# Order of transposes, stores, loads and casts at the end of block 0 and in the two batches after it

## The chip, the cores and the metric

The kernel runs on one core of one Trainium2 chip. The metric is the device time of one execution in microseconds (us): the median of several runs. One more execution is taken by the hardware profiler, and all durations of single instructions come from it. TensorE is PE here, VectorE DVE, ScalarE ACT, GpSimd POOL, and SyncE, which only issues DMAs, SP.

## The reference

A retention layer over 8 batches, 8 heads, 576 tokens and a head size of 64, and then a feed-forward layer with a snake activation on all 4608 tokens:

```python
scores = (1/8) * q @ k.T
ret = (scores * Dmat) @ v          # Dmat[h, i, j] = gamma_h ** (i - j) for i >= j, else 0
x = ret, as 4608 tokens by 512 (batch and position by head and size)
h = x @ w_in                       # 512 by 2048
s = sin(alpha * h)
g = h + s * s / (alpha + 1e-9)
out = g @ w_out                    # 2048 by 512
```

Inputs and output are float32.

## The kernel before, in words

Each batch b has an object `at[b]` that does its retention for the first 512 tokens in two halves p of 256; the last 64 tokens of all batches come at the end as block 8. The 512 outputs of a batch, turned so that the features lie on the partitions (`xT`), are block n of the feed-forward layer. Retention of batch n+1 is woven into the feed-forward work of block n.

For one batch and half: `load` (SP, line 121) brings q, k or v in float32, 512 KB each, into one of six buffers. `cast` (line 181 for q and k, 102 or 104 for v) makes float16 on DVE, ACT or POOL and multiplies in powers of gamma. q and k must be turned so that the head size lies on the partitions (`qT`, `kT`). That is done in one of two ways: on PE with `turn` (line 215, eight 128x128 transposes into a PSUM bank) and two copies `take` (lines 102 and 104), as for batches 0 and 1; or, from batch 2 on, with `crossed` (line 205), a DMA transpose that SP issues. `scores` (line 363) and `masked` (line 375, DVE) make the masked scores, `outer` (line 298) the sums of k and v, `take_sum` and `next_sum` (102, 327), `more` (344, 345) and `to_state` (332) the running state, `values` (line 406) and `add_states` (428) the output, which `keep` (102 or 104) writes to `xT`. The two parts of `values` use the rows of PE in turns at one bank, so the second must come after the first: either PE drains, or an engine relays it. With `relay=A_` an empty instruction on ACT waits for the last matmul of the first part, and the second part waits for ACT (line 250).

For one block and one of 16 columns fc of 128: `project` (line 541) is four matmuls into a bank, `sine` (549, ACT), `square` (558 on ACT, 560 on DVE or POOL), and `product` (565, DVE), which writes `gT` and frees the bank. In blocks 0 and 1 the second matrix follows as `gemm2(n, u, bank)` (line 587): u is 4c + part, c one of four groups of 128 tokens, and part a quarter of w_out: each call multiplies by the four rows fk = 4 part to 4 part + 3, and four calls make one result, which `finish` copies (102 or 104) and SP stores (line 580, two stores of 128 KB). So `gemm2(0, 4)` and `gemm2(0, 12)` and `gemm2(0, 0)` use w_out's first quarter, `gemm2(0, 5)` and `gemm2(0, 13)` the second. The quarters come by `load_w_out(g)`, issued by POOL (line 95) ahead of its squares. `weigh` and the class `Quarters` serve blocks 2 to 8, which make the second product with seven multiplications instead of eight.

The order of the work is written out by hand: each engine's instructions, DMA issues too, stand in the order of the calls, and an instruction that must wait holds up all behind it on its engine. `told(x, eng)` is an empty instruction on `eng` that waits for x. Two of them matter here: POOL waits for the second half of `cast(1, "k", 0)` on DVE, and SP waits for `at[1].masked(0, 0)` ahead of the loads of batch 2.

PSUM has eight banks: h0, h1, h2, op of one bank each and m0, m1 of two. `project(0, 11, "op")` and then `gemm2(0, 4, "op")` use the same bank, so the second waits for `product(0, 11)`; `project(0, 12, "h2")` and `gemm2(0, 12, "h2")` likewise with `product(0, 12)`.

Of the kernel before, what the change touches and what calls it, by code (L numbers as in the profile page):

```python
# [18 lines left out]
def kernel(  # L19
# [68 lines left out]
    V, A_, G_ = nc.vector, nc.scalar, nc.gpsimd  # L88
# [5 lines left out]
    def load_w_out(g):  # L94
        nc.gpsimd.dma_start(w_out16[:, 4 * g : 4 * g + 4, :], w_out_r[:, 4 * g : 4 * g + 4, :])
# [42 lines left out]
    def cast(b, nm, p, eng, ys=(0, 1)):  # L138
        t_ = raw[b, nm, p]
        if (b, nm, p) not in half:  # L140
            if p < 2:
                if nm == "k":
                    d_ = work.tile([P, 16 * D], F16, tag=f"k16{slot(b, p)}", bufs=1, name="k16")
                elif nm == "q":
                    n = order_of_q.index((b, p)) % 3 if b < 5 else 1 - p
                    d_ = work.tile([P, 16 * D], F16, tag=f"q16{n}", bufs=1, name="q16")
                else:
                    d_ = work.tile([P, 16 * D], F16, tag="v16", bufs=4, name="v16")
                d_ = (
                    d_.rearrange("p (h r d) -> p h r d", r=2, d=D)  # L150
                    if nm == "v"
                    else d_.rearrange("p (a r t d) -> p a r t d", a=4, r=2, t=2)
                )
            elif nm == "v":
                d_ = work.tile([P, H, D], F16, tag="vs16", bufs=B // 2, name="vs16")
            else:
                tag, n = ("qks16", 2) if b % 4 == 0 else (f"k16{int(nm == 'q')}", 1)
                d_ = work.tile([P, 4, 2, D], F16, tag=tag, bufs=n, name=nm + "s16")
            half[b, nm, p] = d_
        dst = half[b, nm, p]  # L160
        if p == 2:
            if nm == "v":
                copy(eng, dst.rearrange("p h d -> p (h d)"), t_.rearrange("p h d -> p (h d)"))
            else:
                eng.tensor_tensor(
                    dst.rearrange("p a t d -> p t a d"),
                    t_.rearrange("p (t a) d -> p t a d", t=2),
                    fac_s[nm].rearrange("p (t a) -> p t a", t=2).unsqueeze(3).to_broadcast([P, 2, 4, D]),
                    MULT,
                )  # L170
        elif nm == "v":
            h0, h1 = 4 * ys[0], 4 * ys[-1] + 4
            copy(
                eng,
                dst[:, h0:h1].rearrange("p h r d -> p (h r d)"),
                t_[:, h0:h1].rearrange("p h x -> p (h x)"),
            )
        else:
            a0, a1 = 2 * ys[0], 2 * ys[-1] + 2
            n = 2 * (a1 - a0)  # L180
            return eng.tensor_tensor(  # L181
                dst[:, a0:a1].rearrange("p a r t d -> p t (a r) d"),
                t_.rearrange("p (t a) x -> p t a x", t=2)[:, :, a0:a1].rearrange("p t a (r d) -> p t (a r) d", r=2),
                fac["halved k" if nm == "k" and b >= HALVED else nm]
                .rearrange("p (t x) -> p t x", t=2)[:, :, 2 * a0 : 2 * a1]
                .unsqueeze(3)
                .to_broadcast([P, 2, n, D]),
                MULT,
            )
# [19 lines left out]
    def turn(b, nm, p, tag, ys=(0, 1)):  # L209
        if (b, nm, p) not in trs:  # L210
            trs[b, nm, p] = psum.tile([P, 1024], F16, tag=tag, bufs=1, name="tr")
        tr, x = trs[b, nm, p], half[b, nm, p]
        for a in range(2 * ys[0], 2 * ys[-1] + 2):
            for r in range(2):
                matmul(
                    tr[:, 256 * a + 128 * r : 256 * a + 128 * r + 128],
                    x[:, a, r].rearrange("p t d -> p (t d)"),
                    ident,
                    start=(a == 0 and r == 0), stop=True, is_transpose=True, skip_group_check=True,
                )  # L220

    def take(b, nm, p, eng, ys=(0, 1)):
        d_ = new_T(b, nm, p).rearrange("p x n -> p (x n)")
        cols = slice(512 * ys[0], 512 * ys[-1] + 512)
        copy(eng, d_[:, cols], trs[b, nm, p][:, cols])
# [22 lines left out]
    def told(last, eng):  # L248

        mark = eng.nop()  # L250
        order(mark, last)
        return mark
# [280 lines left out]
    def project(n, fc, tag, part=None):  # L533

        if n not in gT:
            gT[n] = work.tile([P, 2, FC, 256], F16, tag="gT", bufs=2, name="gT")
        if (n, fc) not in hps_of:
            hps_of[n, fc] = [bank(tag), None]
        cols = PART[part]
        for a in range(KT):  # L540
            matmul(  # L541
                hps_of[n, fc][0][:, cols], w_in16[:, a, fc * P : (fc + 1) * P], xs[n][:, a, cols],
                start=(a == 0 and part != 1), stop=(a == KT - 1), skip_group_check=True,
            )
# [9 lines left out]
    def square(n, fc, eng):  # L554
        s_t = hps_of[n, fc][1]
        ss_t = work.tile([P, 512], F16, tag="ss", bufs=4, name="ss_t")
        if eng is nc.scalar:
            nc.scalar.activation(ss_t, s_t, mybir.ActivationFunctionType.Square)  # L558
        else:
            eng.tensor_tensor(ss_t, s_t, s_t, MULT)  # L560
        hps_of[n, fc][1] = ss_t

    def product(n, fc):
        hps, ss_t = hps_of.pop((n, fc))
        nc.vector.scalar_tensor_tensor(  # L565
            gT[n][:, :, fc, :], ss_t.rearrange("p (t n) -> p t n", t=2), inva[:, fc : fc + 1],
            hps.rearrange("p (t n) -> p t n", t=2), MULT, ADD,
        )
# [7 lines left out]
    def finish(n, c, eng=None, cols=slice(0, 512), issue=(nc.sync, nc.sync)):  # L576
        osb = work.tile([P, 512], F32, tag="osb", bufs=4, name="osb")
        copy(eng or nc.scalar, osb[:, cols], ops[n, c, cols.start][:, cols])
        for r in range(2):
            issue[r].dma_start(rows_of(n, c)[r, :, cols], osb[halves(r), cols])  # L580

    def gemm2(n, u, tag, cols=slice(0, 512)):
        c, part = divmod(u, 4)
        if (n, c, cols.start) not in ops:
            ops[n, c, cols.start] = psum.tile([P, 512], F32, tag=tag, bufs=1, name="ops")
        for fk in range(4 * part, 4 * part + 4):
            matmul(  # L587
                ops[n, c, cols.start][:, cols], gT[n][:, c // 2, fk, c % 2 * P : c % 2 * P + P], w_out16[:, fk, cols],
                start=(fk == 0), stop=(fk == FC - 1), skip_group_check=True,
            )  # L590
# [102 lines left out]
    at = [Attention(b) for b in range(B)]  # L693
# [52 lines left out]
    with tc.manual_schedule():  # L746
# [139 lines left out]
        project(0, 10, "m0")  # L886
        sine(0, 10)
        square(0, 10, G_)
        told(cast(1, "k", 0, V, (1,)), G_)
        project(0, 11, "op")  # L890
        sine(0, 11)
        square(0, 11, A_)
        product(0, 10)
        product(0, 11)
        project(0, 12, "h2")
        sine(0, 12)
        square(0, 12, G_)
        project(0, 13, "h0")
        sine(0, 13)
        square(0, 13, A_)  # L900
        cast(1, "q", 0, G_)
        load_w_out(2)
        load_w_out(3)
        product(0, 12)
        project(0, 14, "h1")
        sine(0, 14)
        square(0, 14, A_)
# [1 line left out]
        project(0, 15, "m1")  # L909
        sine(0, 15)  # L910
        square(0, 15, A_)
        gemm2(0, 4, "op")
        turn(1, "k", 0, "m0")
        take(1, "k", 0, V, (0,))
        take(1, "k", 0, V, (1,))
        product(0, 14)
        product(0, 15)
        gemm2(0, 12, "h2")
        gemm2(0, 0, "h0")
        turn(1, "q", 0, "m0")  # L920
        take(1, "q", 0, A_, (0,))
        take(1, "q", 0, A_, (1,))
        at[0].to_state(3, G_)
        gemm2(0, 5, "op")
        gemm2(0, 13, "h2")
        at[1].scores(0, 0, "m0")
        at[1].scores(0, 1, "m1")
# [42 lines left out]
        at[1].outer((1,), "m0")  # L970
        at[1].next_sum(2)
        at[1].to_state(2, V)
        at[1].take_sum(3, A_)
        at[1].values(1, False, "m1", relay=A_)
        gemm2(0, 7, "op")
        at[1].values(1, True)
        at[1].add_states(1)
        at[1].keep(1, A_)
        finish(0, 1)
        cast(2, "k", 1, V, (1,))  # L980
        cast(2, "k", 0, V)
        crossed(2, 0, "k")
        crossed(2, 1, "k")
        at[1].more(3)
        at[1].to_state(3, G_)
        cast(2, "v", 0, G_)
# [13 lines left out]
        product(1, 0)  # L1000
        cast(2, "q", 0, V)
        crossed(2, 0, "q")
        load(3, "k", 1)
        finish(0, 0)
        square(1, 1, A_)
        project(1, 2, "m1", 0)
        project(1, 2, "m1", 1)
# [3 lines left out]
        project(1, 3, "h0")  # L1011
        sine(1, 3)
        crossed(2, 1, "q")
        load(3, "q", 1)
        load(3, "v", 0)
        load(3, "k", 0)
# [99 lines left out]
        sine(1, 15)  # L1116
        cast(3, "v", 1, A_, (0,))
        cast(3, "k", 0, V, (1,))
        load(4, "k", 0)
        crossed(3, 0, "k")  # L1120
        cast(3, "v", 0, G_, (0,))
        cast(3, "v", 1, G_, (1,))
        at[2].more(3)
# [390 lines left out]
```

## Time and profile before

| what | value |
|---|---|
| time, median of 3 runs | 295.11 us (294.53 to 295.81) |
| the profiled execution: its own time | 296.25 us |
| the profiled execution: span from first to last instruction | 294.5 us |
| PE busy | 280.7 us, 95% |
| DVE, ACT, POOL busy | 217.1, 211.3, 207.9 us |
| granted clock of PE | 1.0 throughout |
| DMA queue of SP (q1) | 114528 packets, 45.04 MB |
| DMA queue of POOL (q0) | 4224 packets, 4.19 MB |

Times in the views are us from the start of the span. A row of a timeline is start, length, engine, line, operation, output and inputs with their shapes, count, and in brackets the idle time ahead of it and what ended it. A row of the chain of waits is start, length, what. A row of a stage is its bounds, its length, then the busy time of PE, PEld (weight loads), DVE, ACT and POOL with their counts, then the granted clock, the mean busy share of the 16 DMA engines (it can pass 1 where packets overlap), and GB/s.

### The profile page before, as it was taken

The page shows a single profiled execution, that of the slowest core. Times are in us where ns is not written, and L with a number is a line of the kernel's source. Part 1 is how long each engine was busy: PE and PEld are TensorE (multiplying, and loading weights), DVE is VectorE, ACT ScalarE, POOL GpSimd, SP SyncE. Part 2 cuts the span into 40 slices and gives each one's busy share as a digit, 9 for nine tenths or more (in the row PEclk, how much of TensorE's full clock was granted, in tenths as well). Part 3 has the DMA queues.
Part 4 walks back from the last instruction along what each step waited for, and adds up shares of the span by engine and source line. Part 5 has one row for each costly group of instructions (what it writes and reads, how often), then busy time and mean ns, then how long its engine had stood idle before and what let it go on. Part 6 is the DMA issues. An engine that isn't in the chain of part 4 may idle for free.

```text
span 294.5 us, 8771 instructions
## 1 busy us (share of the span) xinstructions
PE 280.7 (95%) x3611; PEld 184.3 (63%) x3611; DVE 217.1 (74%) x299; ACT 211.3 (72%) x343; POOL 207.9 (71%) x198
## 2 busy tenths in 40 slices
PE   6799999989799999999999999999999999999993
PEld 5574455566544666676666666666666666665782
DVE  3859859999666689989686967686778495747861
ACT  3859733976849898787777778787868879887600
POOL 4888868999999989999997799679915800460000
PEclk9999999999999999999999999999999999999999
DMA  7999999999997887978798785778657101311225
GB/s 225 291 250 223 280 238 296 215 188 296 224 261 249 112 191 175 273 181 184 175 251 165 164 231 129 93 162 182 141 114 168 43 4 38 71 38 27 59 47 119
DMA packets 119159, 49.89 MB, mean 169 GB/s; under 512 B 69824, under 2 KB 118096, under 8 KB 119120
## 3 DMA queue, kind: packets, MB, share of 16 engines
q1 hardware_dynamic: 114528, 45.04, 65.2%
q0 software_dynamic: 4224, 4.19, 8.6%
q8 instruction: 28, 0.46, 0.7%
q10 hardware_dynamic: 368, 0.11, 0.2%
q14 instruction: 11, 0.09, 0.1%
HBM read 36.74 MB, written 9.44 MB: 157 GB/s over the span
## 4 chain that ended last, share of the span: by engine, by line
PE 75%; POOL 7%; DVE 6%; DMA 4%; ACT 3%; issue 2%; SPq 1%; ACTq 0%; POOLq 0%
PE hps L541 32%; PE hps L658 29%; PE ops L587 6%; DVE gT L565 2%; POOL T L608 2%; PE o L406 2%; PE sc L363 2%; DMA k<-in_k_dram 2%; DVE ret L375 2%; DMA qT<-q 2%; DVE k L181 2%; ACT s_t L549 1%; SPq L121 1%; POOL q L181 1%; PE kv L298 1%
## 5 line engine op out<-in xcount | busy, mean ns | idle before, releaser
L565 DVE SCALAR_TENSOR_TENSOR gT<-ss_t,inva,hps 128x512 f16<-128x512 f16 x144 | 105.2, 744 | 41.0 <-ACT ss_t L558 39.3
L549 ACT ACTIVATE s_t<-hps,alpha_t 128x512 f16<-128x512 f32 x144 | 96.5, 681 | 37.4 <-PE hps L541 37.0
L541 PE MATMUL hps<-xT,w_in 128*128 128x512 f16 (+1 forms) x604 | 121.3, 347 | 0.3
L541 PEld LDWEIGHTS <-w_in 128*128 128x128 f16 x668 | 63.7, 98 | 50.4 <-issue 1.2
L558 ACT ACTIVATE ss_t<-s_t 128x512 f16<-128x512 f16 x121 | 75.7, 630 | 3.4
L658 PEld LDWEIGHTS <-gT 128*128 128x128 f16 x656 | 63.9, 98 | 14.5
L630 POOL TENSOR_TENSOR gT<-gT,d 128x1024 f16<-128x1024 f16 x12 | 25.6, 2151 | 26.7 <-PE hps L658 26.0
L658 PE MATMUL hps<-T,gT 128*128 128x256 f16 x336 | 39.8, 273 | 0.0
L375 DVE TENSOR_TENSOR ret<-sc,mask 128x1024 f16<-128x1024 f32 (+1 forms) x32 | 35.0, 1119 | 6.4 <-PE sc L363 6.4
L658 PE MATMUL hps<-w_out,gT 128*128 128x256 f16 x320 | 38.2, 273 | 0.0
L678 DVE TENSOR_TENSOR osb<-osb,hps 128x512 f32<-128x512 f32 x35 | 24.0, 685 | 12.6 <-PE hps L658 11.3
L587 PE MATMUL ops<-w_out,gT 128*128 128x512 f16 x128 | 30.8, 380 | 0.7 <-DVE gT L565 0.7
L636 POOL TENSOR_TENSOR gT<-gT 128x1024 f16<-128x1024 f16 x12 | 25.3, 2128 | 0.0
L181 POOL TENSOR_TENSOR q<-q,cn 128x1024 f16<-128x1024 f32 (+1 forms) x16 | 25.2, 1590 | 0.1
L332 POOL TENSOR_TENSOR s<-kvs,cn 128x256 f16<-128x256 f32 x22 | 14.6, 664 | 8.2 <-ACT kvs L102 7.4
L587 PEld LDWEIGHTS <-gT 128*128 128x128 f16 x128 | 11.8, 98 | 13.1 <-issue 0.9
L345 POOL TENSOR_TENSOR kvs<-s,kvs 128x256 f32<-128x256 f32 x23 | 18.7, 812 | 1.8
L181 POOL TENSOR_TENSOR k<-k,cn 128x1024 f16<-128x1024 f32 (+1 forms) x11 | 18.8, 1709 | 0.0
L102 ACT COPY osb<-hps 128x512 f32<-128x512 f32 (+2 forms) x15 | 8.2, 549 | 13.5 <-PE hps L658 13.3
L102 ACT CAST xT<-o 128x1024 f16<-128x1024 f32 (+1 forms) x14 | 13.8, 989 | 4.0 <-PE o L428 4.0
L344 POOL TENSOR_TENSOR s<-kvs,cn 128x256 f32<-128x256 f32 x23 | 15.5, 673 | 1.6 <-DVE kvs L327 1.4
L541 PE MATMUL hps<-xS,w_in 128*128 128x512 f16 x64 | 15.0, 379 | 0.0
(78 smaller groups left out, 271.1 us busy)
## 6 DMA issues: line engine op xcount, KB each, us to landing
out_dram<-osb SPq DMA_DIRECT2D x70, 128.0 KB, 2.5
q<-in_q_dram SPq DMA_DIRECT2D x16, 512.0 KB, 6.0
k<-in_k_dram SPq DMA_DIRECT2D x10, 512.0 KB, 5.8
v<-in_v_dram SPq DMA_DIRECT2D x10, 512.0 KB, 6.6
k<-in_k_dram SPq DMA_DIRECT2D x24, 128.0 KB, 3.4
v<-in_v_dram SPq DMA_DIRECT2D x24, 128.0 KB, 3.6
w_in<-in_moe_w_in_dram POOLq DMA_DIRECT2D x4, 512.0 KB, 9.1
w_out<-in_moe_w_out_dram POOLq DMA_DIRECT2D x4, 512.0 KB, 9.5
```

The costliest lines, as they stand in the source:

```text
L102: eng.copy(d_, s_)
L181: return eng.tensor_tensor(dst[:, a0:a1].rearrange("p a r t d -> p t (a r) d"), t_.rearrange("p (t a) x -> p t a x", t=2)[:, :, a0:a1].rea ...
L375: made = nc.vector.tensor_tensor(ret.rearrange("p t (z x) -> p (t z) x", z=2)[:, :, 0:n], sc.rearrange("p t (z x) -> p (t z) x", z=2)[:, : ...
L541: matmul(hps_of[n, fc][0][:, cols], w_in16[:, a, fc * P : (fc + 1) * P], xs[n][:, a, cols], start=(a == 0 and part != 1), stop=(a == KT - ...
L549: nc.scalar.activation(s_t, hps, mybir.ActivationFunctionType.Sin, bias=0.0, scale=alpha_t[:, fc : fc + 1],)
L558: nc.scalar.activation(ss_t, s_t, mybir.ActivationFunctionType.Square)
L565: nc.vector.scalar_tensor_tensor(gT[n][:, :, fc, :], ss_t.rearrange("p (t n) -> p t n", t=2), inva[:, fc : fc + 1], hps.rearrange("p (t n) ...
L587: matmul(ops[n, c, cols.start][:, cols], gT[n][:, c // 2, fk, c % 2 * P : c % 2 * P + P], w_out16[:, fk, cols], start=(fk == 0), stop=(fk ...
L630: eng.tensor_tensor(self.part(0, 0, i), self.part(1, 1, i), self.d3[:, 4 * i : 4 * i + 4], SUB)
L636: eng.tensor_tensor(out_, self.part(1, 0, i), self.part(0, 0, i), SUB)
L658: matmul(self.ps[name][:, 256 * m + cols.start : 256 * m + cols.stop], left(j)[:, P * m : P * m + P], right(j)[:, cols], start=(tag is not ...
L678: nc.vector.tensor_tensor(out_, a, self.ps[ps], ADD)
```

## The change

Three groups of moves; no instruction is added or removed but for one copy that goes from ACT to DVE.

Block 0's end: the second half of `cast(1, "k", 0)` on DVE, and POOL's wait for it, move from ahead of products 11 and 10 to behind product 12; product 11 comes ahead of product 10; `load_w_out(2)` comes ahead of that wait, behind square 12; `gemm2(0, 12)` and `gemm2(0, 5)` come ahead of the turn of k, product 14 too; the second take of q goes to DVE.

On DVE, before (from its 16th row on; `k_635` is the cast k of batch 1, the rows of line 565 are products, the first of them up to product 9):

```order
L565 SCALAR_TENSOR_TENSOR gT<-ss_t,inva,hps 128x2x256 x9
L181 TENSOR_TENSOR k_635<-k_361,cn 128x2x4x64 x2
L565 SCALAR_TENSOR_TENSOR gT<-ss_t,inva,hps 128x2x256 x4
L104 COPY kT<-tr 128x512 x2
L565 SCALAR_TENSOR_TENSOR gT<-ss_t,inva,hps 128x2x256 x2
L375 TENSOR_TENSOR ret<-sc,mask 128x1024 x2
```

and now:

```order
L565 SCALAR_TENSOR_TENSOR gT<-ss_t,inva,hps 128x2x256 x9
L181 TENSOR_TENSOR k_635<-k_361,cn 128x2x4x64
L565 SCALAR_TENSOR_TENSOR gT<-ss_t,inva,hps 128x2x256 x3
L181 TENSOR_TENSOR k_635<-k_361,cn 128x2x4x64
L565 SCALAR_TENSOR_TENSOR gT<-ss_t,inva,hps 128x2x256 x2
L104 COPY kT<-tr 128x512 x2
L565 SCALAR_TENSOR_TENSOR gT<-ss_t,inva,hps 128x2x256
L104 COPY qT<-tr 128x512
L375 TENSOR_TENSOR ret<-sc,mask 128x1024 x2
```

Three products now stand between the two halves of the cast, and a copy of qT ahead of the mask product.

Batch 1's end: the first part of `at[1].values(1)`, with its relay on ACT, comes ahead of `take_sum(3)` on ACT. 

Batches 2 and 3, the queue of SP. Before (from its 19th row on; the stores are those of `finish(0, 3)`, `finish(0, 1)` and, the third pair, `finish(0, 0)`; `k_1100` and `k_999` are the cast k of batch 2, halves 0 and 1, `q_1155` and `q_1114` its q, `k_1159` the first load of batch 3):

```order
L580 DMA out_dram<-osb 64x512 x4
L205 DMA_TRANSPOSE kT<-k_1100 128x8x128
L205 DMA_TRANSPOSE kT<-k_999 128x8x128
L205 DMA_TRANSPOSE qT<-q_1155 128x8x128
L121 DMA k_1159<-in_k_dram 128x8x128
L580 DMA out_dram<-osb 64x512 x2
L205 DMA_TRANSPOSE qT<-q_1114 128x8x128
```

and now, where half 0 is `k_1096` and `q_1153`, half 1 `k_999` and `q_1112`, and the load is `k_1188`:

```order
L580 DMA out_dram<-osb 64x512 x2
L205 DMA_TRANSPOSE kT<-k_1096 128x8x128
L580 DMA out_dram<-osb 64x512 x2
L205 DMA_TRANSPOSE qT<-q_1153 128x8x128
L580 DMA out_dram<-osb 64x512 x2
L205 DMA_TRANSPOSE kT<-k_999 128x8x128
L205 DMA_TRANSPOSE qT<-q_1112 128x8x128
L121 DMA k_1188<-in_k_dram 128x8x128
```

Half 0's transposes have moved up past two stores and past half 1's k, and the load has moved down past a pair of stores and half 1's q. In batch 3 the transpose of k, half 0, comes ahead of the first load of batch 4.

The diff, with the calls around it:

```diff
         square(0, 10, G_)
-        told(cast(1, "k", 0, V, (1,)), G_)
         project(0, 11, "op")
         sine(0, 11)
         square(0, 11, A_)
+        product(0, 11)
         product(0, 10)
-        product(0, 11)
         project(0, 12, "h2")
         sine(0, 12)
         square(0, 12, G_)
+        load_w_out(2)
+        product(0, 12)
+        told(cast(1, "k", 0, V, (1,)), G_)
         project(0, 13, "h0")
         sine(0, 13)
         square(0, 13, A_)
         cast(1, "q", 0, G_)
-        load_w_out(2)
         load_w_out(3)
-        product(0, 12)
...
         square(0, 15, A_)
+        product(0, 14)
         gemm2(0, 4, "op")
+        gemm2(0, 12, "h2")
+        gemm2(0, 5, "op")
         turn(1, "k", 0, "m0")
         take(1, "k", 0, V, (0,))
         take(1, "k", 0, V, (1,))
-        product(0, 14)
         product(0, 15)
-        gemm2(0, 12, "h2")
         gemm2(0, 0, "h0")
         turn(1, "q", 0, "m0")
         take(1, "q", 0, A_, (0,))
-        take(1, "q", 0, A_, (1,))
+        take(1, "q", 0, V, (1,))
         at[0].to_state(3, G_)
-        gemm2(0, 5, "op")
         gemm2(0, 13, "h2")
...
         at[1].to_state(2, V)
+        at[1].values(1, False, "m1", relay=A_)
         at[1].take_sum(3, A_)
-        at[1].values(1, False, "m1", relay=A_)
...
         at[1].keep(1, A_)
-        finish(0, 1)
         cast(2, "k", 1, V, (1,))
         cast(2, "k", 0, V)
         crossed(2, 0, "k")
-        crossed(2, 1, "k")
+        finish(0, 1)
...
         crossed(2, 0, "q")
-        load(3, "k", 1)
         finish(0, 0)
+        crossed(2, 1, "k")
...
         crossed(2, 1, "q")
+        load(3, "k", 1)
         load(3, "q", 1)
...
         cast(3, "k", 0, V, (1,))
+        crossed(3, 0, "k")
         load(4, "k", 0)
-        crossed(3, 0, "k")
```

## The prediction

> **What bounds the kernel now.** First the page's line of busy times: it says which engine has no room to spare.
>
> ```profile
> PE 280.7 (95%) x3611; PEld 184.3 (63%) x3611; DVE 217.1 (74%) x299; ACT 211.3 (72%) x343; POOL 207.9 (71%) x198
> ```
>
> PE is busy for 280.7 of 294.5 us. A change that leaves PE's instructions alone, as this one does, can only give back PE's waits or add to them. The view of waits, PE alone, lists them for the whole run; the rows that lie in the part of the program that the change touches:
>
> ```profile
> PE sc L363 <- DMA qT<-q: 2.5, 2, 1.5
> PE ops L587 <- DVE gT L565: 0.7, 1, 0.7
> PE o L406 <- ACTq L250: 0.2, 1, 0.2
> ```
>
> The columns are total, times, longest. Together 3.4 us, 1.1% of the span: that is all that can be won, and the last of them ends at 80.16 us. Behind that PE has no wait that the view names, so what PE gains or loses by 80 us is carried to the end.
>
> **Where the four waits stand.** The timeline of PE:
>
> ```profile
> 32.35 1.02 PE L587 MATMUL ops<-w_out,gT 128*128 128x512 f16 x4 [0.66 <-DVE gT L565]
> 50.09 0.42 PE L406 MATMUL o<-ret,v 64*64 64x128 f16 x16 [0.15 <-ACTq L250]
> 59.52 1.92 PE L541 MATMUL hps<-xT,w_in 128*128 128x256 f16 x16
> 62.45 0.42 PE L363 MATMUL sc<-qT,kT 64*64 64x128 f16 x16 [1.01 <-DMA qT<-q]
> 77.95 0.71 PE L298 MATMUL kv<-v,k 64*64 64x64 f16 x64
> 80.16 0.42 PE L363 MATMUL sc<-qT,kT 64*64 64x128 f16 x16 [1.50 <-DMA qT<-q]
> ```
>
> I follow PE through them and keep its shift against before: plus is later.
>
> **1. Block 0's end, first half: the wait for product 11.** DVE and POOL:
>
> ```profile
> 29.38 1.60 DVE L181 TENSOR_TENSOR k<-k,cn 128x512 f16<-128x512 f32 x2
> 30.90 2.71 DVE L565 SCALAR_TENSOR_TENSOR gT<-ss_t,inva,hps 128x512 f16<-128x512 f16 x4
> 29.86 1.25 ACT L549 ACTIVATE s_t<-hps,alpha_t 128x512 f16<-128x512 f32 x2
> 31.11 1.04 POOL L560 TENSOR_TENSOR ss_t<-s_t 128x512 f16<-128x512 f16 x1 [1.28 <-ACT s_t L549]
> ```
>
> PE ends projection 15 at 32.35 - 0.66 = 31.69 and waits for bank `op`, which product 11 (the second of the four, 30.90 + 2 x 0.66) frees at 32.3. Now one k cast instead of two stands ahead of it, and product 11 ahead of product 10: the cast ends near 30.2, product 11 near 30.9, before PE comes. **The 0.66 is gone.** Product 12 needs square 12, which POOL has so far held back until the second k cast was done; sine 12 ends near 30.5, so square 12 runs 30.6 to 31.6 and product 12 ends at 32.3, before PE asks for bank `h2` at 32.6.
>
> **2. Block 0's end, second half: a wait that takes its place.** PE now issues `gemm2(0,4)`, `gemm2(0,12)` and then at once `gemm2(0,5)`. The first two use w_out's first quarter; the third multiplies by the second quarter, rows 4 to 7, which `load_w_out(1)` brings. Its issue, asked for alone, and its time to landing:
>
> ```profile
> L95 POOL DMA_DIRECT2D w_out<-in_moe_w_out_dram x1: 806/806/806, 26.1 to 26.1; - x1
> DMA to landing us min/median/max: 9.0/9.0/9.0
> ```
>
> It lands at 26.14 + 9.0 = 35.1, and nothing ahead of its issue is changed. Before, `gemm2(0,5)` began behind the turn of q, and the chain of waits shows when:
>
> ```profile
> 32.35 1.02 PE ops L587 x4
> 33.37 0.45 PE tr L215 x8
> 33.82 1.73 PE ops L587 x8
> 35.54 0.45 PE tr L215 x8
> 35.99 1.73 PE ops L587 x8
> 37.72 0.57 PE sc L363 x32
> ```
>
> At 35.99 the quarter had been there for 0.9 us. Now PE reaches it at 31.69 + 2 x 0.87 = 33.4 and has nothing else to do until 35.1: **a new wait of 1.7 us.** From there the rest of this stretch is 3 x 0.87 of gemm2, 2 x 0.45 of turns and 0.57 of scores, 4.1 us, so scores end at 39.2 instead of 38.29: **shift +0.9**. The takes are cover here, not a cost: k's two copies (0.76 together, on DVE) lie beside `gemm2(0,0)`, and q's two, now one on ACT and one on DVE, beside `gemm2(0,13)`; without that cover each would cost up to 0.4. What could bend the landing is `load_w_out(2)`. It was the first of two:
>
> ```profile
> 33.95 1.55 POOL L95 DMA_DIRECT2D w_out<-in_moe_w_out_dram  x2
> ```
>
> It now goes out behind square 12, at 31.6 instead of 33.95; by bounds it moves nothing (it queues behind) or, sharing the engines for the last 2.5 us, makes it up to 1 us later. I take nothing. POOL's cast of q comes 1 us later, near 35, and its turn comes at 37.4, so that costs nothing; `load_w_out(3)` goes out within 0.2 us of before. What follows is read from two stages:
>
> ```profile
> 38.30:50.00 11.70, 11.60 (x204) 5.98 (x204) 9.16 (x13) 3.13 (x5) 7.42 (x10) 1.00 1.09 261
> 50.00:73.35 23.35, 22.11 (x296) 14.94 (x296) 21.59 (x27) 17.73 (x30) 23.03 (x22) 1.00 1.01 238
> ```
>
> From 38.3 to 50 PE (the first busy time) idles 0.1 us, so the shift stays, and DVE, ACT and POOL, which wait for PE's scores and sums there, take it over.
>
> **3. The relay ahead of the last sum.** PE's 0.15 at 50.09 is for ACT's relay, queued behind a copy that waits for DVE. The relay now stands first: **shift +0.8**. The copy itself starts when DVE is done, as before, and the keep after it waits for PE, so nothing new queues there.
>
> **4. qT of batch 2.** SP's issues and what DVE makes for them:
>
> ```profile
> 49.82 4.82 SPq L580 DMA_DIRECT2D out_dram<-osb  x4
> 54.75 2.75 SPq L205 DMA_TRANSPOSE kT<-k  x2
> 57.60 1.25 SPq L205 DMA_TRANSPOSE qT<-q  x1
> 58.90 1.99 SPq L121 DMA_DIRECT2D k<-in_k_dram  x1
> 50.29 2.77 DVE L181 TENSOR_TENSOR k<-k,cn 128x512 f16<-128x512 f32 x2
> 54.57 1.22 DVE L181 TENSOR_TENSOR q<-q,cn 128x1024 f16<-128x1024 f32 x1
> ```
>
> q was ready at 55.8, but its transpose went out at 57.6, behind the second kT. Now kT of half 0 waits for its cast (53.06 + 0.8), two stores follow, and qT goes out as soon as its cast ends (55.8 + 0.8 = 56.6), with 1.3 us less of queue ahead of it. PE is at the scores at 61.44 + 0.8 = 62.2; qT had landed at 62.45 and now lands near 60, at worst at 61.5. **The 1.01 is gone: shift -0.2.** The other kT and qT of batch 2 are asked for only 8 us later, and batch 3's first load, which now goes out behind them, by POOL's cast of k:
>
> ```profile
> 70.31 0.64 PE L363 MATMUL sc<-qT,kT 64*64 64x128 f16 x32
> 67.49 1.04 POOL L181 TENSOR_TENSOR k<-k,cn 128x512 f16<-128x512 f32 x1
> k<-in_k_dram SPq DMA_DIRECT2D x10, 512.0 KB, 5.8
> ```
>
> That load went out at 58.90 and now goes out near 62 and, by the median landing of such loads on the page (third row, the last number), lands near 68; POOL, 0.8 late itself, asks for it at 68.3. So it costs nothing, or at worst 0.5 us of POOL's time, and POOL has that much ahead of SP (step 5). Batch 3's other kT, now ahead of batch 4's first load, comes earlier; PE has no named wait for it today, so it gains nothing.
>
> **5. qT of batch 3, at 80.16, where all this is settled.** POOL makes this q and SP sends it:
>
> ```profile
> 71.45 1.90 POOL L181 TENSOR_TENSOR q<-q,cn 128x1024 f16<-128x1024 f32 x1
> 74.80 1.72 SPq L205 DMA_TRANSPOSE qT<-q  x1
> ```
>
> POOL is busy for 23.03 of the 23.35 us from 50 to 73.35 (the last busy time of that stage), so it takes the 0.8 with it and its cast now ends near 74.2, still ahead of SP's 74.80. From its issue to PE's use of it pass 5.3 us (74.80 to 80.12), because the DMA queue was behind. The view of stages shows how it fell behind, in a stretch ahead of each of the two waits:
>
> ```profile
> 59.40:61.00 1.60, 1.60 (x38) 1.41 (x24) 1.60 (x4) 1.26 (x3) 1.60 (x3) 1.00 0.17 3
> 76.70:78.20 1.50, 1.50 (x42) 1.03 (x42) 0.84 (x3) 1.49 (x4) 1.42 (x3) 1.00 0.99 8
> ```
>
> The last two columns are the DMA share and GB/s. Twice, with transposes under way, the engines moved almost nothing for 1.5 to 1.6 us. The view of DMA for the 0.9 us ahead of the first hole shows what came in there:
>
> ```profile
> q8 instruction: 1, 0.02, 11.4%
> ```
>
> One packet of a queue that carries instructions, and, by its count, PE's: the page has 28 of them, and PE has 7222 instructions, 258 for each. It comes where PE stands in its program, so it moves with PE, not with SP. Near 59.7 (58.9 + 0.8) the new order has the stores of `finish(0,0)`, or the transposes to each side of them, in the queue; I take it that the first hole is missed. Then the queue is 1.6 us ahead, less up to 0.8 because SP now waits for the later k cast: qT lands between 78.5 and 79.4. PE is ready at 80.16 - 1.50 - 0.2 = 78.5. **Shift there -0.8 to -1.6; I take -1.1.** The shift holds to the end, since PE waits for nothing named after it.
>
> [...]
>
> ```profile
> q8 instruction: 28, 0.46, 0.7%
> ```
>
> That is 16.4 KB for each packet. [...]
>
> **The sum.** +0.9 - 0.15 - 1.0 - 0.9 = about -1.1 us, against 296.25 us of the profiled execution (294.5 of span and 1.7 around it). That execution is 1.1 us above the median of 295.11; I put the difference on the median: **294.0 us.**
>
> **Rivals.** *A, slower:* the wait for w_out is not won back. The scores that come 0.9 us late also open SP's loads of batch 2 (SP's first load waits for the mask product), and if the DMA queue, busy from there to 80 us, runs 0.9 late with both holes in it, qT lands at 81.0 and the end comes at 296.0; if the earlier third quarter delays the second by its 1 us as well, 297.0. It decides once the queue, not PE, is what the scores at 80 wait for. For it: the DMA shares of 1.09 and 1.01 in the two stages of step 2. Against it: w_out's third quarter, which shared the engines with those loads, goes out 2.3 us earlier. *B, faster:* both holes are missed, or the scores find qT there: PE alone decides, shift -1.7, 293.4. *C:* w_out's second quarter is there by 33.4; the new wait is not, and PE is 1.7 us further on, bounded then by qT of batch 3: 292.5 to 293.4. The landing row speaks against it. *D, it does nothing:* holes go with transposes wherever these are put, so qT of batch 3 lands at 80.16 as before, whatever PE gained at 62: 295.1.
>
> **Chances.** Forecast 0.45 (293.5 to 294.4), A 0.17, B 0.15, C 0.08, D 0.15. Half a per cent, 1.5 us, is about what a measurement of this kernel can tell from no change. Faster by more than that (below 293.6): B, C and the edge of the forecast, 0.28. Slower by more (above 296.6): the far end of A, 0.12. The rest, 0.60. The range takes in the forecast, D, B and most of A: 292.6 to 296.4.
>
> **What would show it.** The trace after should have PE's first gemm2 at 31.7 without a wait; a wait of PE for w_out of about 1.7 us, ending near 35.1; no wait for ACT near 50; no wait for qT near 62; and between 78 and 80 a wait for qT of batch 3 shorter than 1.50. The stages would show whether a stretch of few GB/s still lies between 58 and 62. The forecast is wrong at step 2 if that wait is absent or longer than 2.5 us, at step 5 if both holes are there again.

## The result and the profile after

| | before | after |
|---|---|---|
| median time, us | 295.09 (294.53 to 296.01) | 297.25 (296.88 to 298.3) |
| ratio, with its 95% interval | | 1.0075 [1.0049, 1.0102] |
| profiled execution, us (its span) | 296.25 (294.5) | 297.32 (295.6) |

The change makes the kernel slower by 2.2 us; 294.0 was forecast. The two profiles alone hide half of that: before's profiled execution lies 1.2 us above its median, after's on it. So a third profile stands beside them below: one more execution of before, unchanged, whose span is 292.3 us (`e8_before_again`).

The view of waits of after, PE alone, has a new row at the top, and the row for qT is there once instead of twice:

```profile
PE ops L587 <- DMA w_out<-in_moe_w_out_dram: 1.7, 1, 1.7
PE sc L363 <- DMA qT<-q: 1.5, 1, 1.5
PE sc L363 <- DVE qT L104: 0.3, 1, 0.3
```

PE's timeline of after at the end of block 0. The first gemm2 comes at 31.55 without a wait, `gemm2(0,5)` waits until 35.20, and the scores that stood at 37.65 before stand at 39.34, 1.69 us later:

```profile
31.55 1.97 PE L587 MATMUL ops<-w_out,gT 128*128 128x512 f16 x8
35.20 1.02 PE L587 MATMUL ops<-w_out,gT 128*128 128x512 f16 x4 [1.67 <-DMA w_out<-in_moe_w_out_dram]
36.06 0.61 PE L215 MATMUL tr<-ident,k 128*128 128x128 f16 x8
36.51 1.03 PE L587 MATMUL ops<-w_out,gT 128*128 128x512 f16 x4
37.61 0.61 PE L215 MATMUL tr<-ident,q 128*128 128x128 f16 x8
39.34 0.64 PE L363 MATMUL sc<-qT,kT 64*64 64x128 f16 x32 [0.27 <-DVE qT L104]
```

The chain of waits of after through the same stretch: what stands between the landing of w_out's second quarter and the end of those scores.

```profile
26.17 8.99 DMA w_out<-in_moe_w_out_dram
35.16 0.04 issue
35.20 1.02 PE ops L587 x4
36.22 0.45 PE tr L215 x8
36.67 0.86 PE ops L587 x4
37.53 0.08 issue
37.61 0.62 PE tr L215 x8
38.23 0.02 issue
38.25 0.59 ACT qT L102
38.84 0.02 issue
38.87 0.43 DVE qT L104
39.30 0.04 issue
39.34 0.64 PE sc L363 x32
```

The quarter lands at 35.16, as forecast (35.1). Behind it one group of `gemm2(0,13)` was counted on the path, and the takes of q beside it. On the chip the takes are the path: ACT 0.59, then DVE 0.43, one after the other.

PE's timeline of after further on:

```profile
63.13 0.42 PE L363 MATMUL sc<-qT,kT 64*64 64x128 f16 x16
79.05 0.71 PE L298 MATMUL kv<-v,k 64*64 64x64 f16 x64
81.27 0.42 PE L363 MATMUL sc<-qT,kT 64*64 64x128 f16 x16 [1.51 <-DMA qT<-q]
```

The same rows of the second execution of before:

```profile
61.36 0.42 PE L363 MATMUL sc<-qT,kT 64*64 64x128 f16 x16
77.35 0.71 PE L298 MATMUL kv<-v,k 64*64 64x64 f16 x64
77.91 0.42 PE L363 MATMUL sc<-qT,kT 64*64 64x128 f16 x16
```

The second execution of before has neither of the two waits that the change was forecast to win back. Against it, PE in after is 1.77 late at the first row and 1.70 at the second: the 1.69 of block 0's end, carried on. The wait for qT then adds 1.5, and that wait also stood in the profile shown with the prediction.

### The profile page after: what moved, and what is told of

It is laid out like the page before. It is cut to its first block, busy times and chain, and to the rows that moved or that the text cites. A ratio compares the mean times of both kernels' runs of the same rounds, so it can differ in the third digit from the quotient of the medians.

```text
span 295.6 us, 8771 instructions
## 1 busy us (share of the span) xinstructions
PE 281.6 (95%) x3611; PEld 184.5 (62%) x3611; DVE 218.1 (74%) x300; ACT 210.6 (71%) x342; POOL 207.3 (70%) x198
## 3 DMA queue, kind: packets, MB, share of 16 engines
HBM read 36.74 MB, written 9.44 MB: 156 GB/s over the span
## 4 chain that ended last, share of the span: by engine, by line
PE 72%; DMA 9%; POOL 7%; DVE 4%; ACT 3%; issue 2%; SPq 2%; ACTq 0%; POOLq 0%
PE hps L541 32%; PE hps L658 29%; PE ops L587 5%; DMA w_out<-in_moe_w_out_dram 3%; POOL T L608 2%; DMA q<-in_q_dram 2%; PE sc L363 2%; DMA k<-in_k_dram 2%; PE o L406 2%; DMA qT<-q 2%; SPq L121 2%; ACT s_t L549 1%; DVE gT L565 1%; POOL q L181 1%; DVE ret L375 1%
```

## The experiments

All marks in us of each profile's span. "Scores" is the start of batch 1's first scores after the start of the first projection. That start differs from one execution to the next, so the difference is the mark to compare: the first projection starts at 17.3 to 17.5 in most of these profiles and at 18.3 to 18.6 in those of e6, e9 and e10, where PE's granted clock was at half for about 3.3 us ahead of it (the row is in the last section). "Wait at 80" is PE's wait for batch 3's qT. The ratio is to before, with its 95% interval.

| kernel | median | ratio | scores | wait at 80 | span |
|---|---|---|---|---|---|
| before (as shown / again) | | | 20.34 / 20.33 | 1.50 / none | 294.5 / 292.3 |
| after (as shown / again) | 297.25 | 1.0075 [1.0049, 1.0102] | 22.00 / 22.01 | 1.51 / 1.0 | 295.6 / 295.1 |
| e1_end_alone | 296.6 | 1.0062 [1.0033, 1.0091] | 21.89 | 1.0 | 294.9 |
| e2_dma_alone | 295.61 | 1.0020 [0.9998, 1.0043] | 20.33 | 1.3 | 293.8 |
| e3_gemm5_late | 295.48 | 1.0020 [0.9995, 1.0044] | 20.10 | 1.4 | 293.8 |
| e10_gemm5_third | 296.1 | 1.0048 [1.0023, 1.0074] | 20.71 | 1.3 | 295.3 |
| e7_takes_act | 297.4 | 1.0102 [1.0050, 1.0154] | 21.99 | 1.5 | 295.5 |
| e6_best | 295.54 | 1.0017 [0.9993, 1.0042] | 20.22 | 0.4 | 293.8 |
| e9_products_alone | 294.91 | 1.0004 [0.9986, 1.0023] | 20.23 | none | 294.1 |
| e11_pool_later | 295.0 | 1.0002 [0.9987, 1.0016] | 20.32 | none | 293.3 |
| e13_load_late | 295.2 | 1.0009 [0.9983, 1.0035] | 20.32 | 2.2 | 296.1 |
| e14_load_early | 295.36 | 1.0012 [0.9988, 1.0036] | 20.11 | 1.1 | 293.7 |

### Which part costs: block 0's end or SP's order

`e1_end_alone` is before with the change of block 0's end alone (line 889 to the turn of q, as in the diff above). `e2_dma_alone` is before with the moves of SP alone:

```diff
-        finish(0, 1)
...
-        crossed(2, 1, "k")
+        finish(0, 1)
...
-        load(3, "k", 1)
         finish(0, 0)
+        crossed(2, 1, "k")
...
         crossed(2, 1, "q")
+        load(3, "k", 1)
...
-        load(4, "k", 0)
         crossed(3, 0, "k")
+        load(4, "k", 0)
```

`e3_gemm5_late` is after with one call back where it was:

```diff
         gemm2(0, 12, "h2")
-        gemm2(0, 5, "op")
         turn(1, "k", 0, "m0")
...
         at[0].to_state(3, G_)
+        gemm2(0, 5, "op")
         gemm2(0, 13, "h2")
```

`e4_before_nops` was to move the packets of the instruction queue that step 5 weighed, with nothing else changed:

```diff
+        for _ in range(96):
+            nc.tensor.nop()
         keep_busy(16, "h0", 256)
```

Expected of the four:

> The kernel before with the change at block 0's end alone; relay and DMA orders as before. Theory (the loss is made at block 0's end: PE meets w_out's second quarter 1.7 us too early, and the two takes of q, on two engines, run one after the other): PE waits 1.6 to 1.8 us for w_out, the scores of batch 1 start 1.5 to 1.7 us late, and the time is 1 to 2.5 us above before. Rival (the loss comes from the new order of transposes, stores and loads): within 0.7 us of before, since a late PE only finds its transposes ready.

> The kernel before with the new order of SP's transposes, stores and loads alone. Theory: the wait for qT of batch 2 near 62 us (1.0 us) shrinks or goes, the wait for qT of batch 3 near 80 us stays or grows by what was won, and the time is 0 to 1 us below before. Rival (the loss is the DMA order's): 1 to 2.5 us above before.

> The changed kernel with gemm2(0, 5) put back to its place behind the turn of q; everything else as changed. Theory: PE's wait for w_out is gone, the scores of batch 1 start 0.3 us early to 0.2 us late against before, and the time is 1 to 2.5 us below the changed kernel, so from 1 us below before to 0.3 us above. Rival: as the changed kernel, 1.5 to 2.5 us above before.

> The kernel before with 96 empty instructions on PE at its start, where PE has nothing to do; no order is changed. They move every later fetch of PE's instructions 96 places earlier in the program, by the trace of before to 51.0, 62.5 and 74.6 us instead of 58.9, 65.8 and 76.5, mostly out of the transposes of batches 2 and 3. Theory of the holes (a fetch amid transposes stops the DMA engines for 1.5 us): the stretches of under 10 GB/s at 59.4 to 61.0 and 76.7 to 78.2 are gone or moved, the waits for qT at 62 and 80 shrink by 1 us or more together, time 0.5 to 2 us below before. Rival (the holes go with the transposes or with the loads behind them): holes and waits as before, time within 0.5 us.

Block 0's end alone costs 0.62%, 1.8 us; SP's order alone 0.2%, with an interval that just reaches no change; it had been expected 0 to 1 us below before. Their sum, 0.82%, is the whole (0.75%) within the intervals. Moving the one call `gemm2(0,5)` back takes after from 1.0075 to 1.0020. PE's timeline of e1:

```profile
35.01 1.02 PE L587 MATMUL ops<-w_out,gT 128*128 128x512 f16 x4 [1.55 <-DMA w_out<-in_moe_w_out_dram]
39.16 0.64 PE L363 MATMUL sc<-qT,kT 64*64 64x128 f16 x32 [0.27 <-DVE qT L104]
```

It is after's picture, 0.1 us shorter. PE's timeline of e3:

```profile
31.68 1.98 PE L587 MATMUL ops<-w_out,gT 128*128 128x512 f16 x8
35.32 0.61 PE L215 MATMUL tr<-ident,q 128*128 128x128 f16 x8 [0.34 <-POOL q L181]
37.58 0.64 PE L363 MATMUL sc<-qT,kT 64*64 64x128 f16 x32
```

In e3 the wait for product 11 is gone and none for w_out comes: half of the 0.66 goes to a wait for POOL's cast of q, which now ends later, and scores stand 0.24 earlier than before, the largest gain that block 0's end shows in any profile. e4 failed: the compiled program has none of the 96 instructions, so this is before once more (295.7, ratio 1.0008). Its profile is of use as such: no wait at 62, 1.5 us at 80.

### How much of the loss is the wait, and how much the takes

`e10_gemm5_third` is after with the call one place later, `e7_takes_act` after with both takes of q on ACT again:

```diff
         gemm2(0, 12, "h2")
-        gemm2(0, 5, "op")
...
         gemm2(0, 0, "h0")
+        gemm2(0, 5, "op")
         turn(1, "q", 0, "m0")
```

```diff
         take(1, "q", 0, A_, (0,))
-        take(1, "q", 0, V, (1,))
+        take(1, "q", 0, A_, (1,))
```

`e12_after_again` is after without an edit, for the spread of its marks.

> The changed kernel with gemm2(0, 5) behind gemm2(0, 0), ahead of the turn of q: PE reaches it about 1.3 us later, near 34.8. Theory (what costs is the time by which PE comes ahead of w_out's landing at 35.1): its wait for w_out is 0.2 to 0.5 us in place of 1.7, the scores of batch 1 start 0.9 to 1.5 us earlier than the changed kernel's 39.34, and the time is 0.8 to 1.8 us below the changed kernel. Rival (the DMA order is what costs): as the changed kernel.

> The changed kernel with both takes of q on ACT, as before. Theory (DVE's copy waits for ACT's, so the split runs one after the other, behind product 15): the scores of batch 1 wait no longer than 0.1 us and start within 0.3 us of the changed kernel's 39.34; time 0 to 0.4 us below the changed kernel. Rival (the split is what makes the changed kernel slow): 1 us or more below it.

> The changed kernel, unchanged, profiled once more. Theory: the wait for w_out is there again, 1.5 to 1.8 us, the scores of batch 1 start near 39.3, and PE comes to the scores of batch 3 near 79.7, later than the 77.9 at which the kernel before started them in its second profile; the wait for qT there may be shorter or longer than the 1.51 us of the first profile.

PE's timeline of e10:

```profile
36.60 1.02 PE L587 MATMUL ops<-w_out,gT 128*128 128x512 f16 x4 [0.63 <-DMA w_out<-in_moe_w_out_dram]
39.20 0.64 PE L363 MATMUL sc<-qT,kT 64*64 64x128 f16 x32 [0.27 <-DVE qT L104]
```

With the call one place later the wait shrinks from 1.67 to 0.63, scores come 1.29 earlier (20.71 against 22.00) and the median falls by 1.15 us (0.8 by the ratios); with it back in its old place (e3) they fall by 1.90 and 1.77 (1.6 by the ratios). So time follows the start of these scores, by 0.6 to 0.9 us for each microsecond. Which engine does the second take does not matter: in e7, with both on ACT, scores wait 0.30 for ACT instead of 0.27 for DVE (at most 0.1 was expected), and the time is not below that of after. The takes are on the path because only one group of gemm2 is left behind the turn of q, where before there were two. e12 repeats the marks of after (w_out 1.7, scores 22.01) and has 1.0 us at 80.

### Are the savings there at all

`e8_before_again` is before without an edit. `e9_products_alone` takes out the wait for product 11 and nothing else; `e6_best` was built as the version that should beat both, with that wait gone, product 10 behind the cast and the relay of step 3:

```diff
         square(0, 10, G_)
-        told(cast(1, "k", 0, V, (1,)), G_)
...
-        product(0, 10)
         product(0, 11)
+        product(0, 10)
...
         square(0, 12, G_)
+        told(cast(1, "k", 0, V, (1,)), G_)
```

```diff
         square(0, 10, G_)
-        told(cast(1, "k", 0, V, (1,)), G_)
...
-        product(0, 10)
         product(0, 11)
...
         square(0, 12, G_)
+        told(cast(1, "k", 0, V, (1,)), G_)
+        product(0, 10)
...
-        at[1].take_sum(3, A_)
         at[1].values(1, False, "m1", relay=A_)
+        at[1].take_sum(3, A_)
```

> The kernel before, unchanged, profiled once more. If the wait for qT near 62 us (1.0 us in the first profile) is there in some executions only, this one may be without it, as the run with dropped empty instructions was; the wait near 80 us is there in all, at 1.0 to 1.5 us.

> The kernel before with one move: products 11 and 10 between the two halves of the k cast, and POOL's wait for the second half behind square 12. PE's order and SP's are as before. Theory (all behind block 0's end moves with PE: PE itself, and by way of POOL's casts the transposes of batch 3): the wait for product 11 is gone, none takes its place, scores of batch 1 start 0.5 to 0.7 us early, and the time is 0.3 to 0.8 us below before. Rival (the DMA queue sets the scores near 80 us by itself): within 0.3 us of before.

> The kernel before with three moves: product 11 directly behind the first half of the k cast, POOL's wait for the second half behind square 12 (product 10 behind the second half), and the relay ahead of the sum on ACT. PE's order is as before, so gemm2(0, 5) stays behind the turn of q. Theory: PE's wait of 0.66 us for product 11 goes and none takes its place, since gemm2(0, 5) is reached at 35.2, when w_out's second quarter has landed; scores of batch 1 start 0.5 to 0.8 us early; of that 0 to 0.9 us is left at the end, because the wait for qT near 80 us takes the rest. Rival (PE at block 0's end has no effect on the end, DMA decides): within 0.3 us of before with the wait near 80 us longer by what was won.

Neither beats before: 1.0004 and 1.0017, both intervals across 1. The chain of waits of e9's profiled execution:

```profile
27.70 9.27 DMA w_out<-in_moe_w_out_dram
36.98 0.04 issue
37.02 1.89 PE ops L587 x8
38.91 0.57 PE sc L363 x32
```

Here the chain no longer comes through DVE's products but through w_out's second quarter: `gemm2(0,5)` begins 0.04 us behind its landing. In before it began 0.85 us behind it (35.99, with a landing at 35.14), and of the 0.66 only 0.1 reaches the scores (20.23 against 20.34). In e6 just as little reaches them (20.22), but not because of w_out: the quarter goes out at 27.16 and takes 9.1, so it is there at 36.3, and PE comes to `gemm2(0,5)` at 36.74. The chain of e6 goes through the products behind the second k cast, which end at 34.53; `gemm2(0,12)` begins at 34.57. In e3 it was POOL's cast of q. So several limits stand a few tenths behind the wait that the change removed, and w_out's landing is one of them. How they lie in a typical execution is not shown: e9's profiled execution took 295.8, 0.9 above its median, and in it and in e6 PE started about 1 us late. What the medians show is that taking out the 0.66 alone wins 0.4 us at most (the lower end of e9's interval).

e8 is the profile used above: 294.04 us, no wait for qT at all, where 1.0 to 1.5 at 80 was expected of every execution.

### What makes the wait at 80 come and go

`e5_before_drains` was the second attempt to move the packets of the instruction queue: 144 drains of PE ahead of its first work.

```diff
+        for _ in range(144):
+            nc.tensor.drain()
         keep_busy(16, "h0", 256)
```

`e11_pool_later` does one of POOL's casts twice, so that POOL comes to batch 3's q about 1 us later:

```diff
         cast(2, "v", 0, G_)
+        cast(2, "v", 0, G_)
```

`e13_load_late` is before with batch 3's first load alone moved; `e14_load_early` is e3 with that load alone moved back:

```diff
-        load(3, "k", 1)
         finish(0, 0)
...
         crossed(2, 1, "q")
+        load(3, "k", 1)
```

```diff
+        load(3, "k", 1)
         finish(0, 0)
...
         crossed(2, 1, "q")
-        load(3, "k", 1)
```

> The kernel before with 144 drains of PE at its start, ahead of the matmuls that only keep PE busy; no order is changed. The 96 empty instructions of the run before this were dropped by the build, so that run was the kernel before once more; drains stay in the program, and all later fetches of PE's instructions come 144 places earlier. By the trace of before that is near 59.4, 74.0, 78.1 and 84.2 us in place of 58.9, 65.8, 76.5 and 82.0. Theory of the holes (a fetch amid transposes stops the DMA engines for about 1.5 us): the transposes of batch 3's half 1, between 75 and 77, meet no fetch, there is no stretch under 10 GB/s in them, and the wait for qT near 80 us shrinks by 1 us or more, time 0.5 to 1.5 us below before. Rival (holes go with the transposes): the wait stays at 1.3 to 1.5 us and the time within 0.5 us.

> The kernel before with one cast of POOL done twice (v of batch 2, half 0, the same values written again), which puts POOL's later work back by 1.2 to 1.6 us and touches no order. Theory (POOL, busy without a break from 50 to 73 us, sets when qT of batch 3 goes out, and so the scores near 80 us): POOL's cast of q ends 1.2 to 1.6 us later than the 73.35 of before, qT goes out as soon as it has ended, the wait of PE near 80 us is 1 to 3 us, and the time is 0.5 to 1.6 us above before. Rival (DMA decides, POOL has slack): within 0.3 us of before.

> The kernel before with one move: batch 3's first load (k, half 1) behind the last transpose of batch 2, as in the change; transposes and stores as before. Theory (that load used to fill the DMA engines while SP waits for POOL's cast of q, and behind it all six loads, two stores and the transposes of batch 3 go out later): qT of batch 3 goes out 0.6 to 1.2 us behind the end of POOL's cast, PE waits 0.8 to 1.6 us for it near 80 us, time 0.2 to 1 us above before. Rival (the order of transposes and stores costs, or nothing does): qT goes out within 0.1 us of the cast's end in the profile, time within 0.3 us of before.

> The changed kernel with gemm2(0, 5) back behind the turn of q and batch 3's first load back to its place ahead of the stores of finish(0, 0); the transposes stay as changed. Theory: the wait for qT near 80 us is 0 to 0.8 us, and the time is 0.3 to 1 us below that of the run with gemm2(0, 5) alone put back (295.48), so at or below before. Rival: as that run, with a wait of 1.0 to 1.5 us.

e5 settles nothing: the drains delay all of PE by 9.7 us (first matmul at 11.02 instead of 1.29), the kernel is 4.35% slower [3.77%, 4.94%], which is more than that delay, and qT of batch 3 is still late by 1.22 us.

e11 shows what a microsecond of POOL costs. PE's timeline:

```profile
75.47 0.31 PE L428 MATMUL o<-qT,s 64*64 64x128 f16 x8 [1.28 <-POOL s L332]
78.94 0.41 PE L363 MATMUL sc<-qT,kT 64*64 64x128 f16 x16
```

PE now waits 1.28 for POOL, and the median does not move (295.0 against 295.04), because qT is there at 78.94 without a wait. The times of e11 lie within 0.6 us (294.67 to 295.29), those of before beside it within 2.3 (293.82 to 296.1). So a typical execution of before seems to have lost about 1 us against e8 (294.04) by then anyway, and a microsecond of POOL hides behind it. The profiles show two places where that can go: the wait for qT at 80, and the late start of the first projection, which goes with the halved clock. The late start is the rarer. Every profile in which the clock was at half for about 3 us has a mean granted clock of 0.994 or less, every other one 0.996 or more; of the 104 timed executions of before beside the experiments, 16 have 0.994 or less (median 296.0), so no more than these can have started late, and the other 88 have a median of 294.7. Whether the wait at 80 is what those have lost is not shown.

POOL and SP show where qT loses its time. POOL's cast of this q in the second execution of before:

```profile
71.42 1.90 POOL L181 TENSOR_TENSOR q<-q,cn 128x1024 f16<-128x1024 f32 x1
```

It ends at 73.32, and SP, in the same execution, is there to send qT at 73.35:

```profile
71.59 1.30 SPq L205 DMA_TRANSPOSE kT<-k  x1
73.35 1.23 SPq L205 DMA_TRANSPOSE qT<-q  x1
```

In after POOL's cast stands 1.70 later, as PE does:

```profile
73.12 1.90 POOL L181 TENSOR_TENSOR q<-q,cn 128x1024 f16<-128x1024 f32 x1
```

But SP is further behind, and qT goes out 0.97 after the cast's end at 75.02:

```profile
74.45 1.43 SPq L205 DMA_TRANSPOSE kT<-k  x1
75.99 1.64 SPq L205 DMA_TRANSPOSE qT<-q  x1
```

The 16 profiles divide by this. In four (e6, e8, e9, e11) SP sends qT 0.03 behind the end of POOL's cast, and PE's wait is 0.4 or none. In the other twelve SP comes 0.36 to 1.45 behind it, and the wait is 1.0 to 2.2. So the wait goes with SP being late; what makes SP late in one execution and not in another stays open.

In SP's timeline of e13 qT goes out 0.46 behind its cast (0.6 to 1.2 was expected), and the issue itself takes 3.02:

```profile
73.74 3.02 SPq L205 DMA_TRANSPOSE qT<-q  x1
```

All seven profiles in which batch 3's first load stands late (e2, e3, e7, e10, e13 and the two of after) have 1.0 to 2.2 us at 80; of the nine with the load early (two of before, e4, e5, e9, e11, e6, e1, e14) three have none. That leans against the later load, though e13's profiled execution, with the 2.2, took 297.79, 2.6 above its median. And the times do not bear it out: e13 is 1.0009 [0.9983, 1.0035], and putting the load back takes e3's 1.0020 only to e14's 1.0012, each interval wider than the difference. Whether SP's order costs the 0.5 us that e2 and e3 suggest, and which of its moves does, stays open.

## Why the prediction was wrong

The sum was +0.9 - 0.15 - 1.0 - 0.9. On the chip it was +1.7, 0, 0 and, open, about +0.5: 2.2 in all.

**Step 1 was right.** The wait for product 11 is gone, PE comes at 31.55 (31.69 forecast). With `gemm2(0,5)` in its old place it brings the scores 0.1 us (e6, e9) to 0.24 (e3) and no time that the medians show, because other limits stand close behind it.

**Step 2 had the mechanism and mis-sized its term: +1.69 instead of +0.9.** The wait is 1.67 (1.7 forecast) and ends at 35.20 (35.1). The stretch behind it was put at 4.1 us and took 4.78 (35.20 to 39.98). The step that failed is "the takes are cover here, not a cost": with `gemm2(0,5)` ahead of the turns, one group of gemm2 (0.87) stands behind the turn of q instead of two, and the two takes with their gaps need 1.10, which is 0.23 more. The rest is PE's own: the first gemm2 after the wait 1.02 instead of 0.87, the second turn 0.62 instead of 0.45 with 0.08 ahead of it, the scores 0.64 instead of 0.57; together 0.47. That the earlier third quarter would hold up the second by up to 1 us did not come about.

**Step 3 won nothing.** The wait for ACT is gone, but in its place the weights of the next matmuls wait for DVE. PE's weight loads in after:

```profile
52.11 0.14 PEld L428 LDWEIGHTS <-s 64*64 64x64 f16 x8 [0.19 <-DVE s L332]
52.35 0.88 PEld L541 LDWEIGHTS <-w_in 128*128 128x128 f16 x9
```

In before the projection stood at 50.66; 52.35 is again 1.69 later. The state that DVE writes (`to_state`, until 52.05) was the next limit: it ends behind the start of the second part of `values` (51.56), and step 3 did not ask for it.

**Step 4 took a wait for the kernel's that was only that execution's.** Its mark came: no wait at 62 in after. But of the profiles with SP's old order there (two of before, e4, e5, e9, e11, e6, e1) only the one shown with the prediction has it. There was nothing to win in a typical execution.

**Step 5 failed at the overlap that it counted on.** "Then the queue is 1.6 us ahead" rested on the first hole being missed. It was not: both holes are there again in after, moved on with the work around them, which the prediction had named as the sign that this step is wrong. Two stages of after:

```profile
62.00:63.50 1.50, 1.50 (x29) 1.11 (x27) 1.50 (x4) 0.64 (x2) 1.50 (x2) 1.00 0.17 9
78.00:79.40 1.40, 1.40 (x54) 1.04 (x53) 0.50 (x2) 1.39 (x4) 1.32 (x2) 1.00 0.24 5
```

9 and 5 GB/s with transposes under way, as rival D had it, and the wait at 80 is 1.51 as before. Nor does such a hole make the wait by itself. The second execution of before has one too, behind the issue of qT, and no wait:

```profile
75.40:76.80 1.40, 1.40 (x11) 0.87 (x9) 1.17 (x2) 1.40 (x3) 1.32 (x3) 1.00 0.18 8
```

PE, POOL's cast and SP's issue in after are 1.7 to 2.6 later than in that execution (e8) by then, so the queue is not ahead of anything.

**The rivals.** A had the right sign, and its landing (qT at 81.0) was near what came (81.27 for the scores); its far end was 297.0. Its reason was half right: the loss of block 0's end is not won back, but not because the DMA queue is late. PE itself is late by 1.7 at 79.05, ahead of any wait for qT. The instruction packets that step 5 weighed are not needed for a hole: e4 and e5, meant to move them, did not separate them from the transposes, but in e13 the queue of instructions moves nothing between 73 and 76.8, and a hole is there with qT's transpose under way. The stage of e13:

```profile
75.40:76.60 1.20, 1.20 (x10) 0.69 (x8) 1.13 (x2) 1.20 (x3) 1.12 (x3) 1.00 0.22 7
```

So this hole goes with the transposes alone, as rival D had it; why it comes is not shown, and in e11 no stretch from 54 to 82 stays below 20 GB/s for as long as 1 us. How long a transpose takes with no other transfer beside it, no run here measured.

The failing was in the reading more than in the sums: the prediction noted that its execution lay 1.1 us above the median, put the difference on the median, and still subtracted 1.0 us for a wait at 62 that only this execution has, and 0.9 us of a wait at 80 that most profiles have and that the new order does not end.

## What to carry to other kernels

Before a wait is counted as something to win, ask whether a typical execution has it: a profile whose own time lies above the median may hold waits that the median does not, and a second profile of the unchanged kernel shows which. Look at the granted clock, stage by stage, before the marks of two profiles are set side by side. When work is moved ahead of a wait, look up when its own data land; a transfer whose landing is fixed (w_out's second quarter here, at 35.16) is a floor, and what is freed ahead of it turns into a wait there, while the cover that the moved work gave behind it is lost. Count copies as hidden only if the work left beside them is longer than they are (here 0.87 of gemm2 stood beside 1.10 of takes).

## What the runs showed of the hardware

One idle time of PE cost more than its own length. In e13 PE stood idle for 2.17 us at 80, and the stages behind it show the granted clock at half (third number from the end):

```profile
80.00:80.80 0.80, 0.61 (x17) 0.44 (x17) 0.00 (x0) 0.00 (x0) 0.80 (x2) 0.52 1.15 348
80.80:82.00 1.20, 1.20 (x6) 0.39 (x4) 1.12 (x1) 0.00 (x0) 1.20 (x2) 0.50 1.24 298
82.00:83.40 1.40, 1.40 (x5) 0.56 (x4) 0.76 (x2) 0.00 (x0) 1.40 (x2) 0.50 1.43 104
83.40:84.20 0.80, 0.80 (x19) 0.31 (x17) 0.00 (x0) 0.19 (x1) 0.80 (x2) 0.97 0.79 172
```

From these scores to the next pair passed 3.71 us (80.19 to 83.90), against 2.17 in after (81.27 to 83.44): 1.5 us on top of the wait. Waits of 1.67 and 1.51 in after left the clock at 1.00 (its stages from 33 to 38 and from 79 to 85). The 2.17 is one execution's: in no other profile did PE wait longer than 1.51 for this qT. Shorter idle times came ahead of a halved clock too: in e6, e9 and e10 it fell ahead of the first projection, with no idle time of PE over 0.8 us since its first transpose. The stage of e9:

```profile
9.60:12.40 2.80, 2.80 (x62) 2.25 (x55) 2.00 (x2) 1.77 (x7) 2.42 (x4) 0.50 1.16 313
```

In it five matmuls of 256 columns took 1.25 us where the second execution of before needs 0.72, and the first projection started at 18.61 instead of 17.32. Most profiles have idle times of this length there and keep the clock at 1.00, so what tips it is not shown.

SP's issue of one and the same transpose took 1.23 to 3.02 us (the rows above), and 144 drains of PE cost 9.7 us, about 68 ns each.
